# Retention and two MLPs on one core: the weights' parts one slot later, the last tile's parts ahead of the chain of g

## The chip, the cores and the metric

One core of one Trainium2 chip runs the whole program. The metric is the device time of one execution in microseconds (us). The kernel before has a median of 586.5 us over 3 runs (586.45 to 586.59).

## The reference

```python
# attention with decay: 16 heads (2 batches x 8), 768 steps, head size 64
state = gamma * state + k_t^T v_t ;  y_t = scale * q_t @ state
x = y as (1536 tokens, 512)
# layer one: w_in 512 x 2048, w_out 2048 x 512
h = x @ w_in ; g = max(h, 0) + log1p(exp(-|h|)) ; x = g @ w_out
# layer two: the same shapes
h = x @ w_in ; r = max(h, 0) ; g = s * (r * r) + b ; out = g @ w_out
```

The weights come as 64-bit floats, all else is 32-bit.

## The kernel before, in words

**Matmuls in three parts.** TensorE multiplies numbers of reduced width (fp32r). So each operand is kept as two tiles, a high part (a copy into fp32r) and a low part (the value minus the high part), and a product takes three matmuls: high by high, high by low, low by high. `split` (L109) makes the two parts: the high one on ScalarE (ACT), the low one on GpSimd (POOL), which cannot read the accumulators in PSUM. Where the value lies in PSUM, VectorE (DVE) makes the low part.

**Weights.** `split_w` (L273) turns a block of 128x512 weights from 64-bit to 32-bit and then into parts. It is a generator that the schedule advances step by step: three DVE steps build the bits (L286, L290, L295), ACT makes a square used against tiny numbers (L293, in step two), step three also issues the next load, step four makes the value `wm` on DVE (L301, which needs the square), and the fifth and last step is `split`: `wh` on ACT (L111), `wl` on POOL (L114). `wm` has two buffers. From the second pair of layer two on, sums of weight blocks are made too: `sums_w` (four POOL operations, L320), and `split_sums` (`sh` on ACT, `sl` on POOL).

**Tokens and layers.** The 1536 tokens are three tiles j = 0, 1, 2 of 512. Layer one runs 48 steps (a block of 128 hidden units for one tile); in the late steps, step s computes h (`h_mm`) and accumulates the output of step s - 3 (`acc_mm`). The output of the last group of blocks is summed with `xa`, in SBUF, and becomes the x of layer two as `xh`, `xl`. Step 47 (NS - 1) ends tile 2; its output is summed in PSUM and split from there by `take_last` (L414).

Layer two works in 8 pairs of blocks. The first pair is `plain(0)`: six slots, each a product of 12 matmuls into one of three banks (h, y, third), then `flat` and `bend`, which make g's parts: on ACT relu L488, square L494, scale and shift L495, `gh` L111, and on POOL `gl` L114; I call these the chain of g. The three first slots also accumulate the last three steps of layer one (`acc_mm`), the fourth begins the accumulation of layer two (`acc_2`) in the same four PSUM banks, of which two are one tile (acc01). The slots are (tile, half): (0,0), (0,1), (1,0), (1,1), (2,0), (2,1). The other seven pairs are `second(p)`, six slots with products of 6 or 12 matmuls. They need sums of x's quarters: `sum_x(k)` for k = 1 to 4 on DVE, in place in `xa`, in the order 1, 3, 2, 4 or an equivalent (2 is built on 1, 4 on 2, and 3 needs the values before 2 and 4), and `parts_x(k)`, their high parts on ACT (L448, L445) and low parts on POOL (L451). The parts of sum 3 are read from two tiles with the tags p5 and u2, which `kept` (L471, on ACT) writes again in the second slot of `second(1)`.

**Order.** Every engine runs its instructions in the order in which the program issues them, written out by hand. In slot (1,0) of the kernel before, the issue order is: the product, `flat` and `bend`, the work on weights, and then `end()`:

```python
for banks in (FIRST, SECOND):
    acc_mm(NS - 1, banks)
    take_last(banks)      # two sums on DVE, two xh on ACT, two xl on DVE
```

In all slots the weights' five steps lie in one slot: two ahead of the accumulation (`go(work, 2)`) and three behind it (`go(work, 3)`). `sum_x(1)` and `sum_x(3)` are in step 47, `sum_x(2)` and `sum_x(4)` in slot (0,0).

Of the kernel before, what the change touches and what calls it, by code (L numbers as in the profile page):

```python
# [7 lines left out]
F32 = mybir.dt.float32  # L8
F32R = mybir.dt.float32r
U32 = mybir.dt.uint32  # L10
AF = mybir.ActivationFunctionType
ALU = mybir.AluOpType
# [12 lines left out]
KC = DM // P  # L25
# [7 lines left out]
FIRST, SECOND = (0, 1), (2, 3)  # L33
# [7 lines left out]
PAIRS = NF // 2  # L41
# [6 lines left out]
def tile_retention_mlps(ctx: ExitStack, tc: tile.TileContext, qk, kv, w1, w2, sb, consts, out):  # L48
    nc = tc.nc
# [18 lines left out]
    def bank(pool, tag):  # L68
        return pool.tile([P, 512], F32, tag=tag, name=tag)
# [195 lines left out]
    bank_2 = []  # L265
# [121 lines left out]
    def acc_mm(s, banks):  # L387
        la, g, j, f4 = steps[s]
        wh, wl = w_t[block(s), 1]
        gh, gl = gg_t[s]  # L390
        if (la, g, j) not in acc_t:
            acc_t[la, g, j] = sums()[0] if acc_t else ac
        parts = ((0, 1), (2,)) if len(banks) > 1 else ((0, 1, 2),)
        for some in parts:
            for cc in banks:
                cs = slice(cc * P, (cc + 1) * P)
                ops = ((wh[:, cs], gh), (wh[:, cs], gl), (wl[:, cs], gh))
                for i in some:
                    nc.tensor.matmul(  # L399
                        acc_t[la, g, j][cc], *ops[i], start=f4 == 0 and i == 0, stop=ends(s) and i == 2  # L400
                    )
# [9 lines left out]
            split(xh[j][:, cc, :], xl[j][:, cc, :], dst, nc.scalar, nc.gpsimd)  # L411


    def take_last(banks):  # L414

        la, g, j, _ = steps[NS - 1]
        ps = [acc_t[la, g, j][cc] for cc in banks]
        for t, cc in zip(ps, banks):
            nc.vector.tensor_tensor(out=t, in0=t, in1=xa[j][:, cc], op=ALU.add)
        for t, cc in zip(ps, banks):  # L420
            nc.scalar.activation(xh[j][:, cc], t, AF.Copy)
        for t, cc in zip(ps, banks):
            nc.vector.tensor_tensor(out=xl[j][:, cc], in0=t, in1=xh[j][:, cc].bitcast(F32), op=ALU.subtract)  # L423

    x_t = {}
    x3 = []
# [42 lines left out]
    def kept(ps, tag):  # L469
        t = late.tile([P, TT], F32, tag=tag, name=tag)  # L470
        nc.scalar.activation(t, ps, AF.Copy)  # L471
        return t
# [7 lines left out]
    def joined(ps, t):  # L480
        c = next_t()
        nc.vector.tensor_tensor(out=c, in0=ps, in1=t, op=ALU.add)
        nc.scalar.activation(c, c, AF.Relu)
        return c

    def flat(ps):
        c = next_t()
        nc.scalar.activation(c, ps, AF.Relu)  # L488
        return c
# [3 lines left out]
    def bend(c, p, half, j):  # L493
        nc.scalar.activation(c, c, AF.Square)  # L494
        nc.scalar.activation(c, c, AF.Identity, scale=sbt[:, 0:1], bias=sbt[:, 1:2])  # L495
        pool, more = (gp, {}) if n_g[0] % 6 < 4 else (late, {"bufs": 2})
        n_g[0] += 1
        gh = pool.tile([P, TT], F32R, tag="gh", name="gh", **more)
        gl = pool.tile([P, TT], F32R, tag="gl", name="gl", **more)
        split(gh, gl, c, nc.scalar, nc.gpsimd)  # L500
        gg_t[p, half, j] = gh, gl

    def acc_2(p, j, half, banks=FIRST + SECOND):
        wh, wl = w_t[NF + 2 * p + half, 1]
        gh, gl = gg_t[p, half, j]
        if (1, p, j) not in acc_t:
            acc_t[1, p, j] = sums()[0]
        for some in ((0, 1), (2,)):
            for cc in banks:
                cs = slice(cc * P, (cc + 1) * P)  # L510
                ops = ((gh[:, cs], wh), (gl[:, cs], wh), (gh[:, cs], wl))
                for i in some:
                    nc.tensor.matmul(  # L513
                        acc_t[1, p, j][cc], *ops[i], start=half == 0 and i == 0, stop=half == 1 and i == 2
                    )
# [9 lines left out]
            nc.sync.dma_start(out=out[r0 : r0 + P, :], in_=dst)  # L525

    NS = len(steps)
    SUMS_AT = {NS - 1: (1, 3)}
    N0 = CPT * HF
    SB = (NU - N0) // HF  # L530
    GS = NTILE * FG
# [26 lines left out]
    def split_next(s):  # L558
        x = nxt[0]
        if x is None or (x[0] < NF + 2 and x[1] < 2 and s < slot_free(*x)) or (NF + 2 <= x[0] and s < NS):  # L560
            return iter(())
        assert x[0] >= NF or s + 1 <= first_use(*x) or s <= min(SB, first_use(*x)), (s, x)
        nxt[0] = next(splits, None)
        if x[1] == 2:
            return sums_w(x[0])
        if x[1] == 3:
            return split_sums(x[0])
        return split_w(*x, pause=True)

    def go(work, n):  # L570
        for _ in range(n):
            next(work, None)
# [43 lines left out]
    work, left = [iter(())], [0]  # L616
# [13 lines left out]
    with tc.manual_schedule():  # L630
# [90 lines left out]
        for s in range(SB, NS):  # L721
# [25 lines left out]
                sum_x(k)  # L747
            go(work, 2)

        def part(p):  # L750
            return split_next(NS + p) if p < PAIRS - 1 else iter(())

        def take(p, j, banks=range(KC)):
            for cc in banks:
# [2 lines left out]
        def plain(p):  # L757

            w = NF + 2 * p

            def slot(j, half, to, accs, sums=(), parts=()):
                work = part(p)
                all_of(to, w_t[w + half, 0], j)
                c = flat(to)
                bend(c, p, half, j)
                go(work, 2)
                accs()
                for k in sums:
                    sum_x(k)
                for k in parts:  # L770
                    parts_x(k)
                go(work, 3)

            def end():
                for banks in (FIRST, SECOND):
                    acc_mm(NS - 1, banks)
                    take_last(banks)

            def sums_0():
                acc_2(p, 0, 1)  # L780
                take(p, 0)

            slot(0, 0, bank(ps_h, "h"), lambda: acc_mm(NS - 3, FIRST + SECOND), sums=(2, 4), parts=(1,))
            slot(0, 1, bank(ps_y, "y"), lambda: acc_mm(NS - 2, FIRST + SECOND))
            slot(1, 0, bank_2[1], end)
            slot(1, 1, bank(ps_h, "h"), lambda: acc_2(p, 0, 0), parts=(2,))
            slot(2, 0, bank_2[1], sums_0, parts=(4,))
            slot(2, 1, bank(ps_y, "y"), lambda: None, parts=(3,))

        def second(p):  # L790

            w = NF + 2 * p
            (ah, al), (bh, bl), (sh, sl) = w_t[w, 0], w_t[w + 1, 0], s_t[w]
            a11, a12 = (ah[:, :KH], al[:, :KH]), (ah[:, KH:], al[:, KH:])
            a22 = bh[:, KH:], bl[:, KH:]
            s1, s2, s3, s4 = ((sh[:, k], sl[:, k]) for k in range(4))
            b11, b21 = ((xh[0][:, k : k + 2], xl[0][:, k : k + 2]) for k in (0, 2))
            b22 = xh[1][:, 2:4], xl[1][:, 2:4]
            t1, t2, t3, n4 = (x_t[k] for k in (1, 2, 3, 4))

            one, other, third = bank(ps_h, "h"), bank(ps_y, "y"), bank_2[1]

            work = part(p)
            six(one, a11, b11, True)
            p1 = kept(one, "p1")
            six(third, a12, b21, True)
            c11 = joined(third, p1)
            go(work, 2)
            acc_2(p - 1, 1, 0)
            bend(c11, p, 0, 0)  # L810
            go(work, 3)

            work = part(p)
            six(other, s1, t1, True)
            p5 = kept(other, "p5")
            six(one, s2, t2, False)
            u2 = kept(one, "u2")
            go(work, 2)
            acc_2(p - 1, 1, 1)
            take(p - 1, 1)  # L820
            go(work, 3)

            work = part(p)
            six(other, s4, b22, False)
            c12 = joined(other, u2)
            six(one, s3, t3, False)
            c22 = joined(one, p5)
            go(work, 2)
            acc_2(p - 1, 2, 0)
            bend(c12, p, 0, 1)  # L830
            bend(c22, p, 1, 1)
            go(work, 3)

            work = part(p)
            six(one, a22, n4, False)
            c21 = flat(one)
            go(work, 2)
            acc_2(p - 1, 2, 1)
            take(p - 1, 2)
            bend(c21, p, 1, 0)  # L840
            go(work, 3)

            work = part(p)
            all_of(third, (ah, al), 2)
            ha = flat(third)
            go(work, 2)
            acc_2(p, 0, 0)
            bend(ha, p, 0, 2)
            go(work, 3)

            work = part(p)
            other = bank(ps_y, "y")
            all_of(other, (bh, bl), 2)
            hb = flat(other)
            go(work, 2)
            for banks in (FIRST, SECOND) if p == PAIRS - 1 else (FIRST + SECOND,):
                acc_2(p, 0, 1, banks)
                take(p, 0, banks)
            bend(hb, p, 1, 2)
            go(work, 3)  # L860

        go(work, 4)
        act_3(NS - 1)
        act_hi(NS - 1)
        act_lo(NS - 1)
# [80 lines left out]
```

## Time and profile before

| | |
|---|---|
| median of 3 runs | 586.5 us |
| the profiled execution | 586.24 us |
| its span, first to last instruction | 584.2 us, so 2.04 us lie around it |
| PE (TensorE matmuls) | 568.8 us busy, 97% |
| DVE | 420.7 us, 72% |
| ACT | 314.8 us, 54% |
| POOL | 238.1 us, 41% |
| granted TensorE clock, mean | 0.993 of full speed |

A share of busy time is a mean over stages with different limits; matmuls are pipelined, so a busy PE need not run at its peak. A wait is shown with what ended it: "[6.62 <-DVE xl L423]" behind an instruction means that its engine stood idle for 6.62 us ahead of it, until the instruction of line 423 on DVE had written xl. In the views over time the first number is the start, the second the duration (of all instructions merged into the row, from the first start to the last end), both in us.

### The profile page before, as it was taken

The numbers are of one execution on the slowest core, as the hardware profiler recorded it, in microseconds if no ns is written. First come the engines' busy times: TensorE is split into PE (matmuls) and PEld (weight loads), VectorE is DVE, ScalarE is ACT, GpSimd is POOL, SyncE is SP. The second block draws the span as 40 slices with busy tenths as digits, with TensorE's granted clock in tenths as the row PEclk, the third lists the DMA queues.
The fourth block names the chain that finished last, engine by engine and source line by source line (L and its number), as shares of the span: only waits on it lengthen the run. The fifth ranks groups of instructions, "written<-read, shape, count | busy, mean of one in ns | idle before, by whom it ended". The sixth has DMA issues, their size and how long they took to land.

```text
span 584.2 us, 7958 instructions
## 1 busy us (share of the span) xinstructions
PE 568.8 (97%) x2986; PEld 466.6 (80%) x2986; DVE 420.7 (72%) x626; ACT 314.8 (54%) x570; POOL 238.1 (41%) x197
## 2 busy tenths in 40 slices
PE   8999999999999999999999599999999999999997
PEld 7777778888888888888888477888888888888885
DVE  4899766788799997999869476666567575756324
ACT  3655564444233233333435577858676767677460
POOL 3447632111110120121533867656474756465030
PEclk9999999999999999999999989999999999999999
DMA  8985212122122121122111113221302131200005
GB/s 326 415 313 201 64 57 88 52 94 72 38 73 72 55 90 37 61 83 72 44 66 37 36 40 105 71 74 38 105 18 94 36 109 36 74 1 0 1 0 215
DMA packets 14869, 50.57 MB, mean 87 GB/s; under 512 B 1776, under 2 KB 1776, under 8 KB 14832
## 3 DMA queue, kind: packets, MB, share of 16 engines
q1 hardware_dynamic: 14832, 50.08, 24.9%
q8 instruction: 23, 0.38, 0.2%
q14 instruction: 14, 0.11, 0.1%
HBM read 46.93 MB, written 3.15 MB: 86 GB/s over the span
## 4 chain that ended last, share of the span: by engine, by line
PE 84%; DVE 7%; ACT 3%; DMA 2%; POOL 2%; issue 1%; SPq 1%; DVEq 0%; POOLq 0%; ACTq 0%
PE acc L513 22%; PE acc L399 21%; PE h L352 12%; PE y L352 9%; PE h L457 6%; PE third L465 4%; PE y L465 3%; PE y L457 3%; PE y L189 2%; DMA kv<-kv 2%; PE third L457 1%; PE s L173 1%; DVE wm L301 1%; DVE xa L438 1%; ACT wh L111 1%
## 5 line engine op out<-in xcount | busy, mean ns | idle before, releaser
L114 POOL TENSOR_TENSOR wl<-wm,wh 128x512 fp32r<-128x512 f32 x64 | 83.3, 1302 | 212.0 <-ACT wh L111 208.9
L522 DVE TENSOR_TENSOR xa<-acc,xa 128x512 f32<-128x512 f32 x84 | 52.4, 683 | 72.0 <-PE acc L513 71.9
L114 POOL TENSOR_TENSOR gl<-c,gh 128x512 fp32r<-128x512 f32 x48 | 63.1, 1315 | 84.2 <-ACT gh L111 70.6
L365 ACT ACTIVATE t<-t 128x512 f32<-128x512 f32 x48 | 30.2, 630 | 102.9 <-DVE t L359 102.7
L513 PE MATMUL acc<-wh,gh 128*128 128x512 f32 x192 | 76.1, 396 | 6.6 <-DVE xl L423 6.6
L513 PE MATMUL acc<-wh,gl 128*128 128x512 f32 x192 | 75.6, 394 | 0.0
L399 PE MATMUL acc<-gh,wh 128*128 128x512 f32 x192 | 75.6, 394 | 0.0
L399 PE MATMUL acc<-gl,wh 128*128 128x512 f32 x192 | 74.8, 390 | 0.0
L111 ACT ACTIVATE wh<-wm 128x512 fp32r<-128x512 f32 x64 | 39.8, 623 | 46.1 <-DVE wm L301 46.0
L399 PE MATMUL acc<-gh,wl 128*128 128x512 f32 x192 | 58.0, 389 | 0.0
L513 PE MATMUL acc<-wl,gh 128*128 128x512 f32 x192 | 53.1, 393 | 0.0
L385 DVE TENSOR_TENSOR gl<-t,gh 128x512 fp32r<-128x512 f32 x40 | 51.8, 1294 | 1.2 <-ACT gh L381 1.2
L513 PEld LDWEIGHTS acc<-wh,gh 128*128 128x128 f32 x192 | 36.5, 190 | 15.5 <-issue 7.0
L293 ACT ACTIVATE wm<-raw 128x512 f32<-128x512 f32 x64 | 42.3, 661 | 8.5 <-POOL wl L114 8.4
L352 PE MATMUL h<-xh,wh 128*128 128x512 f32 x112 | 44.7, 399 | 2.2 <-DVE t L369 1.7
L352 PE MATMUL h<-xl,wh 128*128 128x512 f32 x112 | 43.7, 390 | 0.0
L399 PEld LDWEIGHTS acc<-gh,wh 128*128 128x128 f32 x192 | 36.0, 188 | 8.9 <-DVE xa L409 1.0
L513 PEld LDWEIGHTS acc<-wl,gh 128*128 128x128 f32 x192 | 36.6, 191 | 7.7
L513 PEld LDWEIGHTS acc<-wh,gl 128*128 128x128 f32 x192 | 36.6, 191 | 7.5
L399 PEld LDWEIGHTS acc<-gh,wl 128*128 128x128 f32 x192 | 36.0, 188 | 7.6
L399 PEld LDWEIGHTS acc<-gl,wh 128*128 128x128 f32 x192 | 36.0, 188 | 7.2
L495 ACT ACTIVATE c<-c,sbt 128x512 f32<-128x512 f32 x48 | 39.2, 816 | 1.6
(181 smaller groups left out, 1236.3 us busy)
## 6 DMA issues: line engine op xcount, KB each, us to landing
raw<-w SPq DMA_DIRECT2D x64, 512.0 KB, 3.7
qk<-qk SPq DMA_DIRECT2D x12, 512.0 KB, 8.1
kv<-kv SPq DMA_DIRECT2D x12, 512.0 KB, 8.0
out<-xa SPq DMA_DIRECT2D x12, 256.0 KB, 2.1
cst<-consts SPq DMA_DIRECT2D x1, 518.0 KB, 4.1
cst<-consts SPq DMA_DIRECT2D x1, 256.0 KB, 6.2
sbt<-sb SPq DMA_DIRECT2D x1, 1.0 KB, 9.5
```

The lines of the kernel that those rows point to most:

```text
L111: nc.scalar.activation(hi, src, AF.Copy)
L114: lo_eng.tensor_tensor(out=lo, in0=src, in1=hi.bitcast(F32), op=ALU.subtract)
L293: nc.scalar.activation(m, hw.bitcast(F32), AF.Square)
L352: nc.tensor.matmul(ps, w[:, cc * P : (cc + 1) * P], r[j][:, cc, :], start=i == 0, stop=i == len(ops) - 1)
L365: nc.scalar.activation(l_t[s], l_t[s], AF.Softplus)
L385: (eng or nc.vector).tensor_tensor(out=gl, in0=l_t.pop(s), in1=gh.bitcast(F32), op=ALU.subtract)
L399: nc.tensor.matmul(acc_t[la, g, j][cc], *ops[i], start=f4 == 0 and i == 0, stop=ends(s) and i == 2)
L457: nc.tensor.matmul(ps, w[a][:, k * P : (k + 1) * P], x[b][:, k], start=start and i == 0, stop=i == len(ops) - 1, skip_group_check=True,)
L465: nc.tensor.matmul(ps, w[a][:, k * P : (k + 1) * P], (xh, xl)[b][j][:, k], start=i == 0, stop=i == len(ops) - 1)
L495: nc.scalar.activation(c, c, AF.Identity, scale=sbt[:, 0:1], bias=sbt[:, 1:2])
L513: nc.tensor.matmul(acc_t[1, p, j][cc], *ops[i], start=half == 0 and i == 0, stop=half == 1 and i == 2)
L522: nc.vector.tensor_tensor(out=dst, in0=ps, in1=dst, op=ALU.add)
```

## The change

The weights' last step (`wh`, `wl`) is issued in the slot behind the one that makes the other four steps: `part` keeps the slot's generator and the one of the slot before it, and `end_part` runs the last step of the latter. In `plain` all four steps of a slot now come together, behind the accumulation. In slot (1,0) of `plain(0)` the order becomes product, `end_part`, `end`, then the chain of g. `end` makes the four sums first and then the parts of all four banks. `sum_x(3)` moves from step 47 to slot (0,0), `sum_x(2)` from slot (0,0) to (1,0), and `sum_x(4)` from (0,0) to (1,1).

```diff
-    def take_last(banks):
+    def sum_last(banks):
         la, g, j, _ = steps[NS - 1]
-        ps = [acc_t[la, g, j][cc] for cc in banks]
-        for t, cc in zip(ps, banks):
+        for cc in banks:
+            t = acc_t[la, g, j][cc]
             nc.vector.tensor_tensor(out=t, in0=t, in1=xa[j][:, cc], op=ALU.add)
-        for t, cc in zip(ps, banks):
-            nc.scalar.activation(xh[j][:, cc], t, AF.Copy)
-        for t, cc in zip(ps, banks):
-            nc.vector.tensor_tensor(out=xl[j][:, cc], in0=t, in1=xh[j][:, cc].bitcast(F32), op=ALU.subtract)
+
+    def parts_last():
+        la, g, j, _ = steps[NS - 1]
+        ps = acc_t[la, g, j]
+        for cc in range(KC):
+            nc.scalar.activation(xh[j][:, cc], ps[cc], AF.Copy)
+        for cc in range(KC):
+            nc.vector.tensor_tensor(out=xl[j][:, cc], in0=ps[cc], in1=xh[j][:, cc].bitcast(F32), op=ALU.subtract)
...
-    SUMS_AT = {NS - 1: (1, 3)}
+    SUMS_AT = {NS - 1: (1,)}
...
+        late_work = work
+
         def part(p):
-            return split_next(NS + p) if p < PAIRS - 1 else iter(())
+            nonlocal late_work, work
+            late_work, work = work, split_next(NS + p) if p < PAIRS - 1 else iter(())
+
+        def end_part():
+            go(late_work, 1)
...
             def slot(j, half, to, accs, sums=(), parts=()):
-                work = part(p)
+                part(p)
                 all_of(to, w_t[w + half, 0], j)
-                c = flat(to)
-                bend(c, p, half, j)
-                go(work, 2)
-                accs()
+                if accs is end:
+                    end_part()
+                    end()
+                bend(flat(to), p, half, j)
+                if accs is not end:
+                    end_part()
+                    accs()
+                go(work, 4)
                 for k in sums:
                     sum_x(k)
                 for k in parts:
                     parts_x(k)
-                go(work, 3)
 
             def end():
                 for banks in (FIRST, SECOND):
                     acc_mm(NS - 1, banks)
-                    take_last(banks)
+                    sum_last(banks)
+                parts_last()
...
-            slot(0, 0, bank(ps_h, "h"), lambda: acc_mm(NS - 3, FIRST + SECOND), sums=(2, 4), parts=(1,))
+            slot(0, 0, bank(ps_h, "h"), lambda: acc_mm(NS - 3, FIRST + SECOND), sums=(3,), parts=(1,))
             slot(0, 1, bank(ps_y, "y"), lambda: acc_mm(NS - 2, FIRST + SECOND))
-            slot(1, 0, bank_2[1], end)
-            slot(1, 1, bank(ps_h, "h"), lambda: acc_2(p, 0, 0), parts=(2,))
+            slot(1, 0, bank_2[1], end, sums=(2,))
+            slot(1, 1, bank(ps_h, "h"), lambda: acc_2(p, 0, 0), sums=(4,), parts=(2,))
...
-            work = part(p)
+            part(p)
             six(one, a11, b11, True)
             p1 = kept(one, "p1")
             six(third, a12, b21, True)
             c11 = joined(third, p1)
+            end_part()
             go(work, 2)
             acc_2(p - 1, 1, 0)
             bend(c11, p, 0, 0)
-            go(work, 3)
+            go(work, 2)
... the other five slots of second(p) in the same way
-        go(work, 4)
         act_3(NS - 1)
         act_hi(NS - 1)
         act_lo(NS - 1)
```

## Rows read from the trace of the kernel before

**Rows 1.** The page: TensorE's busy tenths in 40 slices of the span.
```profile
PE   8999999999999999999999599999999999999997
```

**Rows 2.** Waits of PE over the span: total, times, longest, all in us.
```profile
PE acc L513 <- DVE xl L423: 6.6, 1, 6.6
```

**Rows 3.** Busy time by window: stretch, length, engines' busy us, granted clock, DMA.
```profile
328.90:335.60 6.70, 0.08 (x2) 0.07 (x1) 1.48 (x3) 3.54 (x6) 6.58 (x7) 0.87 0.00 0
335.60:341.00 5.40, 5.40 (x13) 3.94 (x14) 4.85 (x8) 4.85 (x8) 1.01 (x1) 0.53 0.00 0
...
361.00:580.00 219.00, 218.96 (x965) 180.98 (x966) 130.57 (x198) 145.37 (x233) 113.91 (x95) 1.00 0.17 56
```

**Rows 4.** The chain that ended last, the stretch behind the long wait.
```profile
335.56 5.48 PE acc L513 x12
341.04 2.73 PE third L465 x12
```

**Rows 5.** Timeline of all engines, 324 to 337 us: around the long wait.
```profile
324.52 0.63 ACT L111 ACTIVATE wh<-wm 128x512 fp32r<-128x512 f32 x1 [3.46 <-DVE wm L301]
...
324.90 1.43 DVE L419 TENSOR_TENSOR acc<-acc,xa 128x512 f32<-128x512 f32 x2 [0.41 <-PE acc L399]
...
325.06 0.58 ACT L488 ACTIVATE c<-y 128x512 f32<-128x512 f32 x1
...
325.61 0.62 PE L399 MATMUL acc<-gh,wl 128*128 128x512 f32 x2
...
327.73 0.58 ACT L488 ACTIVATE c<-third 128x512 f32<-128x512 f32 x1
...
332.06 1.06 ACT L111 ACTIVATE sh<-ws 128x1024 fp32r<-128x1024 f32 x1 [1.59 <-POOL ws L320]
333.03 1.06 ACT L421 ACTIVATE xh<-acc 128x512 fp32r<-128x512 f32 x2
...
334.12 1.29 DVE L423 TENSOR_TENSOR xl<-acc,xh 128x512 fp32r<-128x512 f32 x2 [7.79 <-ACT xh L421]
335.33 1.29 DVE L419 TENSOR_TENSOR acc<-acc,xa 128x512 f32<-128x512 f32 x2
335.56 0.77 PE L513 MATMUL acc<-wh,gh 128*128 128x512 f32 x1 [6.62 <-DVE xl L423]
336.06 1.19 ACT L421 ACTIVATE xh<-acc 128x512 fp32r<-128x512 f32 x2 [1.96 <-DVE acc L419]
...
336.68 1.29 DVE L423 TENSOR_TENSOR xl<-acc,xh 128x512 fp32r<-128x512 f32 x2
```

**Rows 6.** Timeline of all engines, 311 to 321 us: step 47's end and slot (0,0).
```profile
311.82 1.21 DVE L438 TENSOR_TENSOR xa<-xa,xa 128x1024 f32<-128x1024 f32 x1
...
315.73 0.63 ACT L111 ACTIVATE wh<-wm 128x512 fp32r<-128x512 f32 x1 [4.80 <-DVE wm L301]
...
316.44 1.29 POOL L114 TENSOR_TENSOR wl<-wm,wh 128x512 fp32r<-128x512 f32 x1 [5.09 <-ACT wh L111]
...
319.45 0.65 ACT L293 ACTIVATE wm<-raw 128x512 f32<-128x512 f32 x1
...
319.58 3.45 DVE L438 TENSOR_TENSOR xa<-xa,xa 128x1024 f32<-128x1024 f32 x2
319.62 2.33 POOL L114 TENSOR_TENSOR gl<-c,gh 128x512 fp32r<-128x512 f32 x1 [1.90 <-ACT gh L111]
...
320.01 1.05 ACT L448 ACTIVATE x1h<-xa 128x1024 fp32r<-128x1024 f32 x1
```

**Rows 7.** Timeline of all engines, 360 to 361 us: second pair, second and third slot.
```profile
360.39 0.58 ACT L471 ACTIVATE p<-y 128x512 f32<-128x512 f32 x1
...
361.02 0.50 PE L457 MATMUL y<-xh,sh 128*128 128x512 f32 x1 [0.62 <-ACT p L471]
```

**Rows 8.** Timeline of all engines, 392 to 396 us: third pair, second and third slot.
```profile
392.18 2.48 DVE L522 TENSOR_TENSOR xa<-acc,xa 128x512 f32<-128x512 f32 x4 [2.09 <-PE acc L513]
...
395.15 0.39 PE L513 MATMUL acc<-wh,gh 128*128 128x512 f32 x1
```

More of the change, by code (lines that the diff above doesn't have):

```diff
@@ L810, in second @@
             bend(c11, p, 0, 0)
-            go(work, 3)
-            work = part(p)
+            go(work, 2)
+            part(p)
             six(other, s1, t1, True)
@@ L817, in second @@
             u2 = kept(one, "u2")
+            end_part()
             go(work, 2)
@@ L820, in second @@
             take(p - 1, 1)
-            go(work, 3)
-            work = part(p)
+            go(work, 2)
+            part(p)
             six(other, s4, b22, False)
@@ L827, in second @@
             c22 = joined(one, p5)
+            end_part()
             go(work, 2)
@@ L831, in second @@
             bend(c22, p, 1, 1)
-            go(work, 3)
-            work = part(p)
+            go(work, 2)
+            part(p)
             six(one, a22, n4, False)
             c21 = flat(one)
+            end_part()
             go(work, 2)
@@ L840, in second @@
             bend(c21, p, 1, 0)
-            go(work, 3)
-            work = part(p)
+            go(work, 2)
+            part(p)
             all_of(third, (ah, al), 2)
             ha = flat(third)
+            end_part()
             go(work, 2)
@@ L848, in second @@
             bend(ha, p, 0, 2)
-            go(work, 3)
-            work = part(p)
+            go(work, 2)
+            part(p)
             other = bank(ps_y, "y")
@@ L854, in second @@
             hb = flat(other)
+            end_part()
             go(work, 2)
@@ L859, in second @@
             bend(hb, p, 1, 2)
-            go(work, 3)
-        go(work, 4)
+            go(work, 2)
         act_3(NS - 1)
```

## The prediction, made before the run

> **What bounds the kernel now.** I read the page's slices first. TensorE is 90% busy or more in nearly every slice; the exception between start and end is the 23rd, with 5 tenths [rows 1]. A slice is 584.2 / 40 = 14.6 us, so this is 321 to 336 us. The waits of PE come next: one of them is long, 6.6 us at L513 for `xl` of L423 [rows 2]. The windows place it: PE does nothing from 328.9 to 335.6, and then works 5.4 us at a granted clock of 0.53, that is mostly at 1.2 GHz; from 361 to 580 it is busy 218.96 of 219 us at a clock of 1.00 [rows 3]. So TensorE is the bound, and behind 361 us nothing that shortens another engine can gain. In the chain of waits the first 12 matmuls behind the wait take 5.48 us and the next 12 take 2.73 [rows 4]. The stall thus costs 6.62 us of waiting and 5.48 - 2.73 = 2.75 us of slow clock, 9.4 us together.
>
> The timeline shows why the wait is so long [rows 5]. The sums of the first two banks start on DVE at 324.90 and end at 326.33. Their copies to `xh` on ACT start at 333.03 only: ACT has to do the chain of g of slot (0,1) from 325.06, that of slot (1,0) from 327.73, and then `sh`, which waited 1.59 us for POOL's sums of weights. Only then come `xh`, `xl` at 334.12 to 335.41, and the accumulators that PE wants from 335.56 - 6.62 = 328.94 on. ACT was late before that: it waited 4.80 us for `wm` at 315.73 [rows 6] and 3.46 us at 324.52 [rows 5].
>
> **The change, step by step.** Durations are from the profiled execution, which took 586.24 us (span 584.2 and 2.04 around it), 0.26 under the median of the timed runs.
>
> *(a) ACT ahead of slot (1,0).* PE's order up to 328.9 does not change, so its products end when they did. What goes is ACT's two waits for `wm`: with the weights' last step a slot later, g's parts of step 47 and the chain of slot (0,0) no longer queue behind them. A chain of g takes 327.73 - 325.06 = 2.67 us of ACT, a `wh` 0.54 (325.06 - 324.52) [rows 5], a square 0.56 (320.01 - 319.45), an `x1h` about 0.95 [rows 6]. Slot (0,0)'s product ends near 312.6; then chain to 315.3, `wh` 315.85, square 316.4, `x1h` 317.4. Slot (0,1)'s product ends near 318.0: chain to 320.8, `wh` 321.3. ACT is then free 3 to 4 us before the first sum of tile 2 is ready, where before it was at work until 333.
>
> *(b) The sums and parts of tile 2.* On DVE the first two sums end at 326.33. The second pair needs PE's last two matmuls, from 325.61 to 326.23, so it runs at once, 1.29 us, to 327.62 [rows 5]. The four `xl` follow, 1.29 us a pair: 328.91 and 330.20. They need `xh`: ACT can start when the first pair is summed at the latest (326.4), 0.53 each, done by 328.5, and is no hindrance. PE asks for the first two banks (one tile) at 328.94 and gets them some 0.15 us behind 328.91 (before, 335.56 against 334.12 + 1.29 = 335.41 [rows 5]): 329.06. It touches the third bank four matmuls later and the fourth six later; at 2.72 / 12 = 0.227 us each that is 329.97 and 330.42, against `xl` at 329.56 and 330.20. So the wait falls from 6.62 us to about 0.1, and with it goes the slow clock.
>
> *(c) What the chain of slot (1,0) pays.* It now starts behind four `xh`, at 328.5 instead of 327.73, and PE runs 9 us earlier: ACT's slack shrinks. I walk ACT on: chain to 331.2; `sh` to 332.15 (POOL's weight sums, four of about 0.7 us, are long done); slot (1,1) chain 334.8, square 335.4, `x2h` 336.35; slot (2,0) chain 339.0, `wh`, square, `x4h` 341.05; slot (2,1) chain 343.7, `wh`, square, two copies for sum 3, 345.9; `kept` p1 345.9 to 346.5. PE needs the bank of p1 78 matmuls behind 329.06, at 346.75: no wait. Then `joined` and relu (to 347.85), the late `wh` and square (348.95), three operations of g's chain (351.0), p5 to 351.6. PE needs p5's bank 96 matmuls behind 329.06, at 350.85: it waits 0.8 us and goes on at 351.65. Before, the same point was at 361.02, and it waited there 0.62 us [rows 7]. So what is late next is the old small wait, kept.
>
> *(d) The moved sums.* In 328 to 350 DVE gains `sum_x(2)` and `sum_x(4)`, 1.21 us each alone [rows 6], and loses nothing; between the `xl` at 330.2 and the copies of the first accumulators near 337.4 it has 7 us for 2.4 us of sums and 3 us of weight steps. I cost them at nothing; their cover is that PE wants those accumulators at 342.7, with the copies done by 340 to 341. With the cover gone each us is paid in full. `sum_x(3)` lands in 318 to 321, where DVE waits for PE until 324.9. The order 1, 3, 2, 4 keeps their values.
>
> *(e) The weights' last step in `second`.* ACT's `wh` moves from the end of a slot to its place behind the products of the next; same count, same queues, no added DMA. The next load is issued at step three as before. From 361 us on PE has no wait to lose [rows 3], so it gains nothing, and costs nothing as long as it hides beside PE.
>
> *The sum*: 361.02 - 351.65 = 9.4 us off; 586.24 - 9.4 = 576.8 for a profiled execution, and with the 0.26 us by which the timed runs lie above it, 577.1. The bounds: no wait of PE at all in this stretch gives another 0.9 us (576.2). On the other side the walk can slip; half a us per chain of g over the four chains between (b) and p5 is 2 us (579.1).
>
> **A rule of the Trainium skill.** One of the moved sums ran beside POOL: the two rows of 319.58 took 3.45 us, 1.03 more than twice 1.21, and POOL's `gl` beside them 2.33 instead of 1.29 [rows 6]. The Trainium skill, page "SBUF — State Buffer", section "Who interferes with whom", says that a DVE operation with two inputs in SBUF and a GpSimd operation that reads SBUF exclude each other for a whole instruction. By it each collision would cost the loser up to the other's full length, 1.2 to 1.3 us, and not both about 1.0; the trace shows loss on both sides. Sum 4 and POOL's `x2l` would meet near 336.4. By the row two collisions leave POOL a little of its slack in what follows and the time stays 577.1; by the rule, with POOL the loser both times, 2.4 us are gone, all of it, and a third collision makes it some 578.3 (the rival on POOL). No row here shows a full block.
>
> **The rivals.**
>
> *POOL late (578.3).* ACT's p5 and u2 overwrite tiles that POOL's parts of sum 3 still read. By the durations above (`gl` and `wl` 1.29, pairs 2.6, `sl` 2.34) POOL ends the first of them near 347.8 and the second near 349.1, p5 is at 351.0 and u2 at 351.5: 2.4 to 3.2 us of slack. Two collisions as in [rows 6] take 2.1 of it. A third takes the rest and PE pays from there, about 1.2 us for the third and a fourth together: 577.1 + 1.2. For: POOL has g's parts, weights' parts or x's parts to make in each of the six slots of `plain(0)`. Against: of DVE's operations there only the sums read SBUF alone.
>
> *The parts still late (578 to 581).* The first `xl` before started at 334.12, when the second `xh` ended (333.03 + 1.06), not the first; the later one at 336.68 did not wait for its second [rows 5]. If the new `xl` wait for all four `xh`, the first starts at 328.6 and PE at 330.0: 1.0 us, 578.1. If such a wait is long enough to bring the 1.2 GHz back, 2.75 us more: 580.8. The trace has 6.62 us with a fall and 0.62 us without.
>
> *Slower (590).* In `second`, DVE's four copies out of the accumulators stand behind L301, which needs the square, and the square now stands behind a `wh` on ACT. The copies of 392.18 end at 394.66, PE wants the banks at 395.15: 0.49 us of margin. DVE waited 2.09 us for PE ahead of them [rows 8], so L301 can slip 2.6 us before PE pays. There are three such places in six pairs, 18; from 0.52 us of wait at each (L301 3.1 us late) the 9.4 us are gone, at 0.75 us it is 577.1 + 13.5 = 590.6. For: it happens in every pair. Against: one `wh` is 0.63 us, and ACT loses its waits for `wm` there.
>
> *The change does not do what it says (586.5).* A dependence that I don't see keeps the accumulators until the chain of g is done. The code gives no reason for it.
>
> **How the numbers follow.** Forecast 0.72; POOL late 0.10; parts still late 0.11; slower 0.04; no effect 0.03. The predicted time is the forecast's, 577.1. The range of 575.8 to 580.2 takes in the bounds of the walk (576.2 to 579.1), POOL late and most of the second rival; it leaves out some 0.15. A measurement of this kernel tells 0.2% (1.2 us) from no change; all cases but the last two are faster by more: faster 0.93, same 0.03, slower 0.04.
>
> **What would show it.** PE's wait at L513 for `xl` is under 0.5 us, and the granted clock is 1.00 from 325 to 345; the four `xl` stand in one row of DVE, starting near 327.6; ACT's waits for `wm` in 311 to 330 are gone; the first pair of `second` begins near 340 instead of 349. Step (c) is wrong if PE waits over 1.5 us for p1 or p5, step (e) if PE shows waits behind the second pair. The forecast is wrong if the wait at L513 stays above 1 us, or if the stretch from there to the end is longer than 361.02 to the end was.

## The result and the profile after

The changed kernel takes 576.6 us (median of 4 runs, 576.22 to 577.04) against 586.55 us for the kernel before in the same comparison. The ratio is 0.9828, with a 95% interval of 0.9811 to 0.9845. That is faster by 1.7%, or 10 us. The forecast was 577.1 us.

The profiled execution took 576.22 us with a span of 574.4 us; before it was 586.24 and 584.2. The slice with 5 tenths [rows 1] is gone from TensorE's line on the page:

```profile
PE   8999999999999999999999999999999999999997
```

In the waits of PE over the span (total, times, longest, in us) no line with `xl` is left, where [rows 2] had 6.6 us. These are the first and the last of the five that are left; `p` is what the prediction calls p5.

```profile
PE h L352 <- DVE t L369: 1.8, 3, 0.8
...
PE y L461 <- ACT p L475: 0.3, 1, 0.3
```

The windows (stretch, length, busy us of PE, PEld, DVE, ACT, POOL, granted clock, DMA) show PE busy throughout, at a clock of 1.00. [Rows 3] had two stretches here, one without work and one at 0.53. Behind 351 us it is what it was: 219.61 of 220 us, against 218.96 of 219 (the wait for p5 ends at 351.16; from 351.2 to 569.8 us PE is busy 218.58 of 218.60).

```profile
325.00:330.00 5.00, 5.00 (x23) 3.87 (x22) 4.97 (x9) 3.65 (x7) 1.85 (x3) 1.00 0.00 0
330.00:335.00 5.00, 5.00 (x24) 4.15 (x23) 3.14 (x4) 4.87 (x8) 3.89 (x3) 1.00 0.00 0
...
351.00:571.00 220.00, 219.61 (x966) 181.34 (x966) 130.80 (x200) 146.39 (x235) 115.09 (x95) 1.00 0.17 57
```

The chain of waits now runs along PE through the place where [rows 4] had 5.48 us for 12 matmuls, and reaches the second pair at 340.20:

```profile
326.37 2.72 PE h L469 x12
329.09 2.95 PE acc L517 x12
332.04 2.72 PE third L469 x12
...
340.20 1.36 PE h L461 x6
```

The timelines of ACT and of DVE show why. ACT ends the weights' parts of slot (0,1) at 321.32 (320.70 + 0.62), waits 4.97 us for the first sum and makes the four copies at once. The sums end at 327.45, the four `xl` stand behind them in one row. In [rows 5] the copies were split into two pairs that started at 333.03 and 336.06.

```profile
320.70 0.62 ACT L111 ACTIVATE wh<-wm 128x512 fp32r<-128x512 f32 x1
326.29 2.07 ACT L425 ACTIVATE xh<-acc 128x512 fp32r<-128x512 f32 x4 [4.97 <-DVE acc L419]
328.21 0.64 ACT L492 ACTIVATE c<-third 128x512 f32<-128x512 f32 x1
```

```profile
324.82 2.63 DVE L419 TENSOR_TENSOR acc<-acc,xa 128x512 f32<-128x512 f32 x4 [4.53 <-PE acc L399]
327.41 2.48 DVE L427 TENSOR_TENSOR xl<-acc,xh 128x512 fp32r<-128x512 f32 x4
329.81 1.22 DVE L442 TENSOR_TENSOR xa<-xa,xa 128x1024 f32<-128x1024 f32 x1
```

So the time is found around one place. PE reaches the third slot of the second pair, 361.02 before [rows 7], at 351.16 (below): 9.86 us earlier. The spans differ by 9.8 us.

### The profile page after: what moved, and what is told of

It is laid out like the page before. It is cut to its first block, busy times and chain, and to the rows that moved or that the text cites. A ratio compares the mean times of both kernels' runs of the same rounds, so it can differ in the third digit from the quotient of the medians.

```text
span 574.4 us, 7963 instructions
## 1 busy us (share of the span) xinstructions
PE 566.1 (99%) x2986; PEld 465.7 (81%) x2986; DVE 419.7 (73%) x626; ACT 315.0 (55%) x570; POOL 238.1 (41%) x197
## 4 chain that ended last, share of the span: by engine, by line
PE 87%; ACT 5%; DVE 4%; DMA 3%; issue 1%; SPq 0%; DVEq 0%; ACTq 0%
PE acc L399 23%; PE acc L517 21%; PE h L352 12%; PE y L352 9%; PE h L461 6%; PE y L469 4%; PE third L469 4%; PE y L461 3%; PE y L189 2%; DMA qk<-qk 2%; PE third L461 1%; PE s L173 1%; ACT wh L111 1%; DVE a L177 1%; DMA cst<-consts 1%; ACT c L499 1%
```

## The experiments

The prediction had the long wait go because of two edits at once: ACT no longer waits for `wm`, and the chain of g no longer stands in front of tile 2's copies. It did not say how much each is worth, nor whether the moved sums are needed. My theory A was that ACT must merely be free when the first sum is ready, at 325 to 326 us, by whatever edit; the rivals were that one particular edit decides. Each run has its own comparison with the kernel before, which read 585.7 to 586.6 us there.

**The order in slot (1,0) alone.**

```diff
 # in the kernel before; take_last is split into sum_last and parts_last as in the change
-                c = flat(to)
-                bend(c, p, half, j)
+                if accs is end:
+                    end()
+                bend(flat(to), p, half, j)
                 go(work, 2)
-                accs()
+                if accs is not end:
+                    accs()
```

> The kernel before with one edit: in slot (1,0) the sums and parts of tile 2 stand ahead of the chain of g. The weights' last step stays in its slot, x's sums stay where they were. Theory A (ACT was late by two edits' worth: the waits for wm, and the chain in front of the copies): ACT still reaches the copies at 327.7 only, since the chain of slot (0,1) starts at 325.06 behind a wait for wm; the first two copies end near 328.8, their xl near 330.1, PE waits about 1.4 us there, no slow clock; ACT is 1.6 us later than in the changed kernel and still waits for wm behind it, so p1 and p5 cost 1 to 3 us more: 578 to 581 us. Theory B (the order in slot (1,0) alone removes the stall): 576.3 to 577.2 us, PE's wait there under 0.4 us. Theory C (the late weights' step alone does it): 585 to 587 us.

579.17 us, ratio 0.988 (0.9866 to 0.9893). Three quarters of the gain, as theory A had it. In ACT's timeline the copies wait for nothing but the chain of slot (0,1), which a wait of 3.46 us for `wm` still delays:

```profile
324.61 0.64 ACT L111 ACTIVATE wh<-wm 128x512 fp32r<-128x512 f32 x1 [3.46 <-DVE wm L301]
325.15 0.58 ACT L492 ACTIVATE c<-y 128x512 f32<-128x512 f32 x1
...
327.81 2.04 ACT L425 ACTIVATE xh<-acc 128x512 fp32r<-128x512 f32 x4
```

PE waits for the accumulators 1.3 us, and in the second pair 0.6 us each for p1 and p5 (its waits from 300 to 380 us):

```profile
PE acc L517 <- ACT c L492: 1.3, 1, 1.3
PE y L461 <- ACT p L475: 0.6, 1, 0.6
PE h L461 <- ACT p L475: 0.6, 1, 0.6
```

The first line names the ACT operation that came last, not the `xl` on DVE that ended at about the same time.

**The late weights' step without the new order.**

```diff
 # in the changed kernel
-                if accs is end:
-                    end_part()
-                    end()
                 bend(flat(to), p, half, j)
-                if accs is not end:
-                    end_part()
-                    accs()
+                end_part()
+                accs()
```

> The changed kernel with one edit undone: in slot (1,0) the chain of g stands ahead of tile 2's sums and parts again; the late weights' step and the moved sums stay. Theory A: ACT is free from 321.3, PE's product for the chain ends near 323.4, so the chain fits in ACT's idle 5 us, until 326.3, when the copies can start anyway. No stall, and the chain is 2.6 us earlier, so the wait for p5 (0.3 us) goes too: 575.8 to 576.5 us, PE's wait for xl under 0.4 us. Theory B (the order decides): the copies start a chain late, at 328.9 or later, PE waits 2 to 3 us: 578 to 582 us.

576.55 us, ratio 0.9834 (0.9821 to 0.9848): no different from the changed kernel. The new order is not needed once the weights' step is late, since the chain fits into ACT's idle time ahead of the sums (ACT):

```profile
323.69 0.60 ACT L492 ACTIVATE c<-third 128x512 f32<-128x512 f32 x1 [2.13 <-PE third L469]
...
326.51 2.07 ACT L425 ACTIVATE xh<-acc 128x512 fp32r<-128x512 f32 x4
```

One part of my expectation failed: p5 still cost PE 0.2 us. ACT began slot (1,1)'s chain at 329.39 and not at 331.88, but gave the lead back, part of it here (DVE, ACT and POOL in the timeline):

```profile
329.60 2.40 POOL L114 TENSOR_TENSOR sl<-ws,sh 128x1024 fp32r<-128x1024 f32 x1 [1.25 <-ACT sh L111]
330.04 3.05 DVE L442 TENSOR_TENSOR xa<-xa,xa 128x1024 f32<-128x1024 f32 x1
332.27 1.99 POOL L114 TENSOR_TENSOR gl<-c,gh 128x512 fp32r<-128x512 f32 x1 [0.27 <-ACT gh L111]
...
333.12 1.06 ACT L452 ACTIVATE x2h<-xa 128x1024 fp32r<-128x1024 f32 x1 [0.36 <-DVE xa L442]
```

Sum 2, 1.22 us in the changed kernel, stood 3.05 us while POOL's `sl` ran until 332.00.

**The late step in pairs two to eight alone.** `plain`, tile 2's parts and x's sums are those of the kernel before.

```diff
 # in the kernel before: part, end_part and all of second(p) as in the change; plain keeps its two calls
-                work = part(p)
+                part(p)
 ...
                 go(work, 2)
 ...
                 go(work, 3)
```

> The kernel before, with the late weights' step in the pairs two to eight alone; plain(0), tile 2's parts and x's sums as before. Theory A: PE has no wait there to lose, the long stall stays: 585.9 to 587.0 us, 6.6 us of wait for xl and the slow clock behind it. Rival (the late step gains or costs something in the steady pairs that PE's waits don't show): under 585.5 or over 587.5 us.

585.61 us, ratio 0.9993 (0.9983 to 1.0002): no difference that can be told, though the time lies 0.3 us under theory A's range. The wait of 6.6 us is there, and the only other wait of PE that the profile of the kernel before has from 300 to 380 us, p5's 0.6, is gone; theory A had not counted it. This is the whole list for that stretch:

```profile
PE acc L513 <- DVE xl L423: 6.6, 1, 6.6
```

**The late step in `plain(0)` alone.** `second` keeps its five steps in one slot.

```diff
 # in the changed kernel, in second(p); end_part only in its first slot, for the step that plain hands on
             end_part()
             go(work, 2)
             acc_2(p - 1, 1, 0)
             bend(c11, p, 0, 0)
-            go(work, 2)
+            go(work, 3)
```

> The changed kernel with the late weights' step in plain(0) alone; pairs two to eight have all five steps in one slot, as before. Theory A: the whole gain is made ahead of the second pair; there ACT has one wh more in the first slot ahead of p5, so the wait for p5 grows by 0.5 us: 576.3 to 577.5 us. Rival (the late step in the second pair is needed, since ACT has no slack there now): p5 waits for wm too, 578 to 580 us.

577.11 us, ratio 0.9847 (0.9834 to 0.9861). Nearly all of the gain is made ahead of the second pair. The one `wh` more in front of p5 shows as a wait of 0.8 us instead of 0.3:

```profile
PE y L461 <- ACT p L475: 0.8, 1, 0.8
```

**x's sums in their old places.**

```diff
-    SUMS_AT = {NS - 1: (1,)}
+    SUMS_AT = {NS - 1: (1, 3)}
...
-    slot(0, 0, ..., sums=(3,), parts=(1,)) ; slot(1, 0, ..., sums=(2,)) ; slot(1, 1, ..., sums=(4,), parts=(2,))
+    slot(0, 0, ..., sums=(2, 4), parts=(1,)) ; slot(1, 0, ...) ; slot(1, 1, ..., parts=(2,))
```

> The changed kernel with x's sums where they were before: sum 3 in step 47, sums 2 and 4 in slot (0,0). Theory A (the sums are off the path): the sums end near 323.5 on DVE, ahead of tile 2's at 324.8; wm of the first weights is 1.2 us later and costs ACT about 0.4 us, which it has: 576.0 to 576.9 us, PE's wait for xl under 0.4 us. Rival (moving them was needed: two sums in slot (0,0) collide with POOL and hold up wm, and ACT with it): 577.5 us or more, ACT waiting over 1.5 us for wm at 320.

576.53 us, ratio 0.9836 (0.9821 to 0.985). Moving the sums is worth nothing by itself here. Two of them took 4.09 us together beside POOL, and DVE still had half a us to wait for PE's accumulators behind them:

```profile
320.44 4.09 DVE L442 TENSOR_TENSOR xa<-xa,xa 128x1024 f32<-128x1024 f32 x2
325.07 1.44 DVE L419 TENSOR_TENSOR acc<-acc,xa 128x512 f32<-128x512 f32 x2 [0.55 <-PE acc L399]
```

**The late step and nothing else.** The kernel before with `part` and `end_part` in all pairs; the old order, the old `take_last`, the old sums.

```diff
 # in the kernel before; second(p) as in the change
-                work = part(p)
+                part(p)
                 all_of(to, w_t[w + half, 0], j)
-                c = flat(to)
-                bend(c, p, half, j)
-                go(work, 2)
+                bend(flat(to), p, half, j)
+                end_part()
                 accs()
+                go(work, 4)
 ...
-                go(work, 3)
```

> The kernel before with the late weights' step alone, in all pairs: slot (1,0) in its old order, tile 2's parts made two banks at a time as before (sums, xh, xl, then the same for the other two), x's sums in their old places. Theory A: this one edit makes nearly all of the gain. The first two banks are free near 328.8; the third's sum waits behind the first two xl, so its xl ends near 330.6 and PE waits for it and the fourth 0.8 to 1.0 us, less what it then does not wait for p5: 576.3 to 577.6 us. Theory B (the order in slot (1,0) or the four sums ahead of the parts are needed): 579 us or more.

577.27 us, ratio 0.9848 (0.9831 to 0.9864): 9 of the 10 us by one edit. What is missing is mainly a wait of 0.7 us for the third bank, whose sum stands behind the first two `xl`; PE no longer waits for p5 in return.

```profile
330.75 0.50 PE L513 MATMUL acc<-wh,gh 128*128 128x512 f32 x1 [0.70 <-DVE xl L423]
```

**The chain first, the sums back.** The late step and the four sums ahead of the parts stay.

```diff
 # in the kernel of "the late weights' step without the new order"
-    SUMS_AT = {NS - 1: (1,)}
+    SUMS_AT = {NS - 1: (1, 3)}
 ... and the sums of the three slots as in "x's sums in their old places"
```

> The changed kernel with two edits undone: the chain of g ahead of tile 2's parts in slot (1,0), and x's sums in their old places; the late weights' step and the four sums ahead of the parts stay. It tests why the chain-first run kept its 0.2 us wait for p5: there sum 2 stood 3.05 us on DVE beside POOL's sl, and ACT then waited 0.36 us for it and 0.32 us for wm. Theory A (the collision ate ACT's lead): no such waits on ACT in 328 to 346, p5 at least 0.4 us earlier against PE, and no wait of PE in 308 to 380: 575.9 to 576.5 us. Rival (ACT's lead goes in any case, into its waits for PE's products): p5 as late as before, PE waits 0.2 us: 576.4 to 576.8 us.

576.4 us, ratio 0.9823 (0.981 to 0.9837). PE has no wait at all from 300 to 380 us, and p5 is some 0.7 us earlier against PE than in the changed kernel (21.00 us behind the first matmul into tile 2's banks, 329.75 to 350.75, against 21.69, 328.84 to 350.53). ACT did not have to wait for sum 2 or `wm`, so the collision was one cause. The rival is right in part too: 0.99 and 0.63 us of ACT's lead went into waits for PE's products. As a time it can't be told from the changed kernel. In the traces PE needs 34.24 us from the product of slot (1,0) to that of the second pair's fifth slot (326.89 to 361.13), 0.6 us less than the changed kernel's 34.87 (325.98 to 360.85), but that one profiled execution came to the first of these points 0.9 us later.

**What a wait of PE costs.** Four runs put extra sums, which nothing reads, on DVE between the sums and the `xl`:

```diff
     def parts_last():
 ...
+        scr = late.tile([P, TT], F32, tag="p1", name="p1")
+        for _ in range(5):      # 9, 3, 4 in the other three
+            nc.vector.tensor_tensor(out=scr, in0=xa[j][:, 0], in1=xa[j][:, 1], op=ALU.add)
         for cc in range(KC):
             nc.vector.tensor_tensor(out=xl[j][:, cc], in0=ps[cc], ...
```

> The changed kernel with five sums of 512 columns that nothing reads (0.6 us each, into a scratch tile) put on DVE ahead of the four xl, so that PE waits about 3 us for the accumulators. It prices a wait between the 0.3 us and the 6.6 us that the traces have. Theory A (a wait of 3 us costs its length): 3.0 us less the 0.3 us wait for p5: 578.9 to 579.6 us, granted clock 1.00 behind it. Theory B (the clock falls for this wait too): 2.7 us more: 581.5 to 582.5 us, the 12 matmuls behind it take about 5.4 us.

> The same with nine such sums, so that PE waits about 5.4 us. Theory A (it costs its length): 581.3 to 582.0 us. Theory B (the clock falls): 584 to 585 us, 12 matmuls in about 5.4 us.

> The changed kernel with three extra sums ahead of the four xl (0.70 us each in the run with five), so that PE waits 2.0 us (3.4 us in that run, less two sums). It brackets the wait from which the clock falls: 1.3 us did not bring it (slot order alone), 3.4 us did. Theory A (2.0 us costs its length, less the 0.3 us wait for p5): 577.9 to 578.7 us, 12 matmuls behind it in 2.8 us or less. Theory B (the clock falls): 580.4 to 581.5 us, 12 matmuls in about 5.3 us.

> The same with four extra sums, a wait of 2.7 us. Theory A: 578.6 to 579.4 us. Theory B: 581 to 582.2 us.

| extra sums | PE's wait, us | 12 matmuls behind it, us | granted clock in them | time, us | PE's way, over 34.87 us |
|---|---|---|---|---|---|
| 3 | 1.97 | 3.01 | 1.00 | 577.85 | 1.4 |
| 4 | 2.70 | 3.00 | 1.00 | 579.73 | 2.9 |
| 5 | 3.43 | 5.46 | 0.50 | 582.12 | 5.6 |
| 9 | 10.25 | 4.84 | 0.58 | 588.41 | 11.5 |

The last column is PE's way in the traces between the same two points as above, less the changed kernel's. The times come from two comparisons, in which the kernel before read 585.66 us (three and four sums) and 586.26 us (five and nine).

The wait and what follows it, of the run with four (first) and with five:

```profile
331.70 0.47 PE L520 MATMUL acc<-wh,gh 128*128 128x512 f32 x1 [2.70 <-DVE xl L430]
```

```profile
332.35 0.77 PE L520 MATMUL acc<-wh,gh 128*128 128x512 f32 x1 [3.43 <-DVE xl L430]
```

Their windows behind the wait have a clock of 1.00 and of 0.50:

```profile
332.00:338.00 6.00, 6.00 (x28) 4.94 (x27) 5.93 (x6) 4.84 (x8) 5.99 (x4) 1.00 0.00 0
```

```profile
332.30:338.00 5.70, 5.65 (x13) 4.47 (x14) 5.63 (x6) 3.92 (x6) 5.68 (x4) 0.50 0.00 0
```

The run with three came out by theory A, if 0.05 us under its range and with 3.01 us for the 12 matmuls instead of 2.8; the changed kernel's own take 2.95. The one with five came out as theory B had it. The one with four lies between the two ranges, 0.3 us over theory A's. Its profiled execution has the full clock; there PE's way is 2.9 us longer, of which the wait is 2.70 and p5's wait 0.2 more. The other timed execution is 0.6 us longer at a mean clock of 0.996 instead of 0.999; whether the clock fell there for a while stays open. With nine I missed the length of the wait, and with it both ranges: the sums took 10.41 us instead of 6.3, and POOL's next three operations ran beside them.

## Why the prediction was right

*(a) and (b), ACT ahead of slot (1,0), and the parts of tile 2.* As predicted nearly to the tenth: ACT free at 321.3 (forecast 321.3), copies from 326.29 (326.4 at the latest), the first `xl` at 327.41 (327.62), the accumulators free for PE without a wait that the profile would count. Before, ACT waited 8.3 us for `wm` in 311 to 330 (4.80 in [rows 6] and 3.46 in [rows 5]); after, not at all. What I did not see is that (a) does it alone: the late step without the new order gives the same 576.5 us, while the new order alone leaves 2.6 us. The chain of slot (1,0) stood in front of the copies, but was harmful only because it started late.

*The price of the stall.* Both parts were paid back, but the slow clock was priced too high: the 12 matmuls behind the wait still take 2.95 us in the changed kernel, so it gave back 5.48 - 2.95 = 2.53 us and not 2.75. Of the 9.86 us, 9.24 are there at the first matmul of the next accumulation (343.61 before, 334.37 after): the wait and the clock. The other 0.6 us come in the second pair: 0.3 from p5's shorter wait, and 0.3 around p1, where 12 matmuls took 3.03 us before (354.49 to 357.52) and take 2.72 now (345.25 to 347.97), a delay too short for the list of waits.

*(c) What is late next.* It was p5, as forecast, and it costs PE 0.30 us instead of 0.8, the mis-sized term of the sum. PE came to it when forecast (351.16 - 0.30 = 350.86, forecast 350.85), but my walk along ACT had p5 at 351.0 and it came at 350.53. Most of the error was there at the start of the walk: the four copies began at 326.29 and the chain of slot (1,0) at 328.21, 0.48 us for a copy and not 0.53, so that chain was 0.29 us ahead of the forecast's 328.5. The walk from there added little: 0.27 us at the chain of slot (1,1) (331.88, forecast 332.15), 0.37 at p1 (345.53, forecast 345.9), 0.47 at p5.

```profile
345.53 0.59 ACT L475 ACTIVATE p<-h 128x512 f32<-128x512 f32 x1
...
350.53 0.58 ACT L475 ACTIVATE p<-y 128x512 f32<-128x512 f32 x1
```

```profile
351.16 0.50 PE L461 MATMUL y<-xh,sh 128*128 128x512 f32 x1 [0.30 <-ACT p L475]
```

*(d) The moved sums.* Costed at nothing, and worth nothing: 576.53 us with the sums back. They are not free of danger, though; in the chain-first run one stood for 3.05 us.

*(e) The late step in the other pairs.* Nothing that the time can tell: ratio 0.9993 alone, and PE waits for nothing behind 351.5 us. Yet from 360 to 580 us ACT's waits for `wm` went from 20.4 us (11 waits) to 1.2 (5 waits): time that an engine off the critical path gets back is worth nothing. In the first slot of the second pair the late step is worth 0.5 us, the `wh` that no longer stands in front of p5. The rival that ends slower needed DVE's copies to be late; instead they wait longer for PE, 3.36 us against 2.09 in [rows 8]:

```profile
382.36 2.48 DVE L526 TENSOR_TENSOR xa<-acc,xa 128x512 f32<-128x512 f32 x4 [3.36 <-PE acc L517]
```

*The rivals.* POOL late: POOL met x's sums in two of its rows, which each took 2.55 us undisturbed:

```profile
317.96 3.50 POOL L455 TENSOR_TENSOR x1l<-xa,x1h 128x512 fp32r<-128x512 f32 x2
...
336.22 3.31 POOL L455 TENSOR_TENSOR x2l<-xa,x2h 128x512 fp32r<-128x512 f32 x2 [0.19 <-ACT x2h L452]
```

That cost it 1.7 us, and it had the slack: its parts of sum 3 began at 347.02 and 348.27, ended near 349.6, and p5 and u2 (350.53 and 351.01) waited for neither. Parts still late: what I had seen at 334.12, the first `xl` waiting for both copies from the two-bank tile, is there in the order-only run too (its `xl` start at 328.91, behind the second copy), but with ACT on time both copies are done when DVE is. Its second price, 2.75 us for the clock at a wait of 1.0 us, is refuted here: waits of 1.3, 1.97 and 2.70 us in the profiles left it at full speed.

*The rule of the Trainium skill.* I read [rows 6] as a loss on both sides, and took that to differ from the full block that the Trainium skill, page "SBUF — State Buffer", section "Who interferes with whom", states. That reading failed. Taken in order of time those rows are full blocks in turn: the first sum holds POOL's `gl` until about 320.7, `gl` then runs its 1.3 us to 321.95 and holds the second sum, which begins at 320.83 in the chain of waits and ends 1.08 us after `gl`:

```profile
320.83 2.20 DVE xa L438
```

The chain-first run shows it plainly: sum 2, due at 330.04, ends at 333.09, that is 1.09 us after `sl` is done at 332.00; the next `gl`, ready at 332.27, takes 1.99 us and ends 1.2 us after the sum. These runs agree with the Trainium skill there: the loser pays the rest of the other's whole instruction.

## What to carry to other kernels

Where an engine works through its queue in order, as ACT does here, look ahead of the instruction that is late for the waits in its queue, not only for long work: here one conversion that waited for another engine, twice, cost 9 us further down its queue. Deferring such a step by one slot made its input old enough that ACT did not wait for it in this stretch, and that single edit did nearly all of it; the reordering around it would have bought three quarters by itself, and beside the late step it bought nothing that the time can tell. And price a stall of TensorE from the trace with what follows it: of two waits 0.7 us apart in length, only the longer one had its next 12 matmuls at half the clock, 2.5 us on top.

## What the runs showed of the hardware that was not expected

The clock fell for a wait of PE of 3.43 us (granted clock 0.50 in the 12 matmuls behind it) and stayed at 1.00 for profiled waits of 1.3, 1.97 and 2.70 us. A wait of 10.25 us cost no more on top than the one of 3.43: its next 12 matmuls took 4.84 us against 5.46, and the 11.5 us that PE's way is longer are the wait and 1.3 us, against 2.2 us beside the wait of 3.43.

A DVE sum of 1024 columns with both inputs in SBUF took 1.22 us with POOL idle and 3.05 us beside a POOL operation of 2.40 us; two of them took 4.09 us beside POOL's parts. Sums with one input in PSUM did not stretch: the four of L419 took 2.63 us in the changed kernel, where POOL's sums of weights ran beside them.
